# New instruction lists for all engines of a fused threshold-attention and gated-MLP kernel

## The chip, the cores and the metric

The program runs on one NeuronCore of a Trainium2 chip. The metric is the device time of one execution, in microseconds (us). The engines named below are PE (TensorE, matmuls), DVE (VectorE), ACT (ScalarE), POOL (GpSimd) and SP (SyncE, whose queue issues nearly all DMAs). PEld is the loading of matmul weights, which overlaps PE.

## The reference

Two parts, one after the other, for 8 batches of 576 tokens.

```python
# attention: 8 batches, 8 heads, 576 tokens, 64 channels per head
scores = (1 / np.sqrt(64)) * np.matmul(q, k.transpose(0, 1, 3, 2))
thresh = np.max(scores, axis=-1, keepdims=True) - tau          # tau = 0.02
scores = np.where(scores >= thresh, scores, -1e9)
attn = np.exp(scores - np.max(scores, axis=-1, keepdims=True))
attn = attn / (np.sum(attn, axis=-1, keepdims=True) + 1e-09)
x = np.matmul(attn, v)          # heads side by side: (8, 576, 512)
# gated MLP: w_in 512x1024, w_spatial 576x576, w_out 512x512
h = np.maximum(x @ w_in, 0.0)
u, v = h[..., :512], h[..., 512:]
v_n = (v - mean(v)) / np.sqrt(var(v) + 1e-06)                  # over channels
v_s = np.einsum('ts,bsd->btd', w_spatial, v_n) + b_spatial[None, :, None]
out = (u * v_s) @ w_out
```

## The kernel before

**The work.** A batch has 8 heads, taken as 4 pairs, and 18 score steps: four steps of 128 rows for each pair, and a fifth step for every second pair that does the last 64 rows of two pairs. There are 144 steps in all. The MLP of a batch follows its attention, one to three batches later, in between the score steps of later batches.

**The order is written out by hand.** `ORDER` holds four strings of tokens. String 0 is the list for batch 0, string 1 for batch 1, string 2 for batch 2, and string 3 is used for each of batches 3 to 7. `run_token` (line 884) turns a token into instructions. Each engine works through its own instructions in the order of the tokens, and waits where an operand or a buffer isn't ready. A token is a name, a colon and a lag: `es1:2` in the list of batch 5 is done for batch 3. A lag of -1 looks one batch ahead. Tokens for a batch below 0, or done already, are skipped. A `d` in front of an eviction puts it on DVE; without it the eviction is on ACT (`evict`, line 297, reads `on_vector`).

**One score step g**, by token:
- `S` and `Y` (lines 685 and 696): the score matmuls of the step, in two parts, into one of two PSUM slots (`s_ring`, two tiles). `G` between them (line 691) is an empty instruction on POOL that `Y` waits for. So PE's step can't end before POOL's queue has come to `G`.
- `M` (702): DVE takes the negative row maxima, `negm`.
- Then one of two forms, chosen by `ON_ACT`. *ACT form*: `B` (708) shifts `negm` by tau on DVE, `E` and `F` (714, the two heads) write `e` on ACT with Prelu of slope 1e30, which sends all below the threshold far down, and `Z` (737) takes the exponential of both heads on ACT. *DVE form*: `E` and `F` take the exponential on ACT, and `W` (731) is the mask on DVE: one instruction that compares `e` with exp(-tau) and multiplies.
- The slot is free for step g+2 when `E` and `F` of step g are done.

**Around it.** `QA`, `QB`, `QR` turn q, k and the last rows on PE; `qa`, `qb`, `qr` evict them (512, 512 and 128 wide); `kd`, `sq`, `sv` are POOL's copies of them and of q, k and v. `T`, `TR` (742) are the DMA transposes of the probabilities, `X`, `XR` those of the attention output; `XP`/`xp`, `RP`/`rp`, `WS`/`ws` are the same kind of turn on PE, with eviction. `P`/`p` and `R`/`r` are probabilities times v, and the division. `L` are loads; `C..` load and cast the weights.

**The MLP of a batch**: five `v` on PE, each evicted by `ev` on ACT with a sum; `n` (543) makes the mean on POOL, `k` (548) squares and sums on ACT, `N` (554) is four POOL instructions that end in the normalised `vn`. Five `u` with eviction `eu`; five `s` with the gate `es` on DVE; four `o` with eviction `eo` and `OUT`, which stores. `v4` also holds the last rows of the output of the batch before.

**After the lists** comes the tail: all that no list has done for batches 5 and 6 (`left`, line 986), then the MLP of batch 7 (`last_gmlp`, line 762), with eight PSUM banks free for it.

Of the kernel before, what the change touches and what calls it, by code (L numbers as in the profile page):

```python
# [16 lines left out]
    "L1:-1 L7:0 S0:0 G0:0 Y0:0 L0:-1 S1:0 M0:0 G1:0 Y1:0 QA1:0 L8:0 M1:0 E0:0 QR1:0 F0:0 B1:0 qa1:0 W0:0 "  # L17
    "S2:0 E1:0 G2:0 Y2:0 F1:0 dqr1:0 M2:0 Z1:0 S3:0 G3:0 kd1:0 Y3:0 E2:0 T00:0 QB1:0 M3:0 F2:0 qb1:0 B3:0 "
    "W2:0 F3:0 S4:0 E3:0 G4:0 Y4:0 Z3:0 M4:0 S5:0 Ci1:0 G5:0 Y5:0 sq2:0 L4:-1 QR2:0 B4:0 M5:0 Ci2:0 F4:0 "
    "QB2:0 E4:0 Cb0:0 dqb2:0 Z4:0 S6:0 T01:0 dqr2:0 B5:0 G6:0 sv0:0 Y6:0 F5:0 RP01:0 M6:0 QA2:0 E5:0 "  # L20
    "rp01:0 B6:0 qa2:0 QR3:0 E6:0 S7:0 G7:0 F6:0 Y7:0 M7:0 Z5:0 Ci0:0 S8:0 G8:0 kd2:0 L9:0 Y8:0 sq3:0 "
    "Z6:0 B7:0 M8:0 sv1:0 qr3:0 QB3:0 E7:0 RP00:0 B8:0 F7:0 kd3:0 T10:0 Cis1:0 drp00:0 E8:0 S9:0 F8:0 "
    "G9:0 Y9:0 Z8:0 M9:0 S10:0 G10:0 sq0:-1 Y10:0 Z7:0 B9:0 dqb3:0 Cis0:0 Cs1:0 M10:0 F9:0 QA3:0 L6:-1 "
    "R0:0 E9:0 dqa3:0 S11:0 B10:0 r0:0 G11:0 Cbs0:0 F10:0 Y11:0 P00:0 E10:0 M11:0 T11:0 sv2:0 Z9:0 S12:0 "
    "G12:0 sv3:0 B11:0 Y12:0 F11:0 P10:0 M12:0 Cis2:0 E11:0 Z11:0 Ci3:0 p00:0 L3:-1 p10:0 P01:0 Z10:0 "
    "Cs2:0 S13:0 p01:0 G13:0 sq1:-1 B12:0 Y13:0 F12:0 M13:0 T20:0 P11:0 E12:0 Css2:0 XP0:0 p11:0 dxp0:0 "
    "XP1:0 B13:0 E13:0 dxp1:0 QA0:-1 S14:0 F13:0 L2:-1 G14:0 Cis3:0 qa0:-1 Y14:0 L5:-1 QR0:-1 M14:0 "
    "QB0:-1 qr0:-1 Css4:0 XR0:0 Z12:0 S15:0 dqb0:-1 G15:0 F14:0 kd0:-1 Y15:0 P20:0 M15:0 E14:0 T21:0 "
# [1012 lines left out]
```

## Time and profile before

| | |
|---|---|
| Three runs | 450.50, 450.74, 450.67 us, median 450.67 us |
| Profiled execution | 450.5 us, of which 448.5 us is the span from the first instruction to the last |
| Granted TensorE clock | 0.996 of full speed |
| PE busy | 416.1 us (93%) |
| DVE busy | 400.8 us (89%) |
| ACT busy | 388.6 us (87%) |
| POOL busy | 176.9 us (39%) |

One instruction `M` per step marks the batches. The first `M` begins at 8.6 us; batches 1 to 7 begin theirs at 57.2, 108.7, 162.2, 213.1, 264.2, 315.2 and 366.5 us, and the last `M` ends at 414.8 us. The stretch from there to 448.5 us is called the tail here. Busy time counts an engine's instructions once where they overlap. A group of instructions is given with its count, the mean duration of one in ns, and the idle time of its engine just before it.

### The profile page before, as it was taken

How to read it: one execution, taken by the hardware profiler on the slowest of the kernel's cores; microseconds unless marked ns; L12 is line 12 of the kernel's file. 1: busy time of each engine (PE TensorE's matmuls, PEld its weight loads, DVE VectorE, ACT ScalarE, POOL GpSimd, SP SyncE). 2: the span in 40 equal slices, each digit the busy share in tenths (PEclk: the TensorE clock that was granted, in tenths of full speed). 3: DMA queues.
4: the chain of work that ended last, by engine and by line, in shares of the span. 5: the costliest groups of instructions: out<-in, count | busy, mean ns of one | idle time of the engine just before them, and what ended most of it. 6: DMA issues, size and time to landing. Idle time of an engine off the chain costs nothing.

```text
span 448.5 us, 12858 instructions
## 1 busy us (share of the span) xinstructions
PE 416.1 (93%) x5035; PEld 260.2 (58%) x5035; DVE 400.8 (89%) x615; ACT 388.6 (87%) x649; POOL 176.9 (39%) x403
## 2 busy tenths in 40 slices
PE   6776879998999899999999999999999999999995
PEld 4455556565656665666565666566665666566542
DVE  5868889899999889999999999999989999999673
ACT  3897989998989899999899988999899998999351
POOL 1256333583225724354333533255333523344021
PEclk9989999999999999999999999999999999999999
DMA  7999899899999989999999999999899996896713
GB/s 206 277 245 204 230 235 184 140 206 211 214 153 235 229 175 209 198 226 237 189 193 209 248 186 184 233 217 239 187 199 213 265 179 107 161 198 122 176 36 107
DMA packets 222556, 88.15 MB, mean 197 GB/s; under 512 B 193568, under 2 KB 218272, under 8 KB 222496
## 3 DMA queue, kind: packets, MB, share of 16 engines
q1 hardware_dynamic: 221840, 86.45, 93.5%
q8 instruction: 40, 0.66, 0.6%
q0 software_dynamic: 160, 0.52, 0.3%
q10 hardware_dynamic: 496, 0.36, 0.2%
q14 instruction: 20, 0.16, 0.1%
HBM read 32.79 MB, written 9.44 MB: 94 GB/s over the span
## 4 chain that ended last, share of the span: by engine, by line
PE 48%; DVE 24%; ACT 18%; issue 6%; POOL 2%; DMA 1%; ACTq 0%; POOLq 0%; DVEq 0%
PE s L678 20%; DVE negm L705 13%; ACT e L722 6%; ACT e L719 5%; PE f L605 5%; PE f L329 4%; PE f L576 4%; DVE p L734 3%; PE f L529 3%; PE f L381 3%; DVE xn L390 2%; ACT p L739 2%; DVE negm L711 2%; PE f L514 1%; PE f L634 1%
## 5 line engine op out<-in xcount | busy, mean ns | idle before, releaser
L705 DVE TENSOR_REDUCE negm<-s 128x2 f32<-128x1152 f32 x144 | 194.5, 1351 | 19.8 <-PE s L678 16.4
L678 PE MATMUL s<-qkT 64*64 64x160 f32 (+1 forms) x2304 | 173.2, 416 | 12.3 <-ACT e L719 7.6
L678 PEld LDWEIGHTS s<-qkT 64*64 64x64 f32 x2304 | 107.4, 132 | 67.8 <-ACT e L719 17.1
L719 ACT ACTIVATE e<-s,negm 128x576 f32<-128x576 f32 x166 | 115.3, 744 | 19.0 <-DVE negm L711 11.3
L722 ACT ACTIVATE e<-s,negm 128x576 f32<-128x576 f32 x122 | 85.8, 756 | 7.4 <-DVE negm L705 7.1
L734 DVE SCALAR_TENSOR_TENSOR p<-e,ctau 128x1152 bf16<-128x1152 f32 x61 | 86.7, 1422 | 3.5 <-ACT e L722 3.2
L739 ACT ACTIVATE p<-e 128x1152 bf16<-128x1152 f32 x67 | 78.3, 1173 | 0.4
L215 POOL CAST v<-vl 128x512 bf16<-128x512 f32 x32 | 21.0, 658 | 79.0 <-PE s L678 72.8
L381 PE MATMUL f<-v,pT 128*128 128x65 bf16 x1008 | 44.6, 194 | 0.0
L381 PEld LDWEIGHTS <-pT 128*128 128x128 bf16 x1024 | 41.6, 98 | 2.4 <-issue 0.4
L545 POOL TENSOR_SCALAR nmean<-sm 128x1 f32<-128x1 f32 (+1 forms) x35 | 16.1, 468 | 55.5 <-PE s L678 34.5
L390 DVE TENSOR_TENSOR xn<-f,r 128x256 bf16<-128x256 f32 (+1 forms) x93 | 35.4, 380 | 2.9
L605 PE MATMUL f<-wsT,vn 128*128 128x512 bf16 x135 | 33.6, 380 | 0.0
L576 PE MATMUL f<-xT,w_in 128*128 128x512 bf16 x120 | 30.8, 380 | 0.6 <-DVE xn L390 0.3
L376 PE MATMUL f<-v,pT 128*128 128x130 bf16 x126 | 27.7, 220 | 2.1 <-DVE r L388 1.5
L192 POOL COPY qn<-ql 128x512 f32<-128x512 f32 x31 | 20.1, 648 | 21.3 <-PE s L678 20.5
L561 POOL TENSOR_SCALAR vn<-vrel,rs,nm 128x512 bf16<-128x512 f32 (+1 forms) x35 | 26.8, 767 | 3.8
L529 PE MATMUL f<-w_in,xT 128*128 128x512 bf16 x112 | 27.9, 379 | 0.2 <-ACT vrel L537 0.2
L551 ACT ACTIVATE sq<-vrel,nmean 128x512 bf16<-128x512 f32 (+1 forms) x35 | 25.8, 739 | 1.7 <-POOL nmean L545 1.6
L634 PE MATMUL f<-w_o,gT 128*128 128x512 bf16 x100 | 25.0, 380 | 1.4 <-ACT qkT L309 1.4
L341 POOL COPY qkT<-qkT 64x64 f32<-64x64 f32 x32 | 7.5, 235 | 40.7 <-PE s L678 21.0
L711 DVE TENSOR_SCALAR negm<-negm 128x2 f32<-128x2 f32 x83 | 22.0, 265 | 1.7
(158 smaller groups left out, 570.8 us busy)
## 6 DMA issues: line engine op xcount, KB each, us to landing
vl<-in_v_dram SPq DMA_DIRECT2D x16, 512.0 KB, 4.9
kl<-in_k_dram SPq DMA_DIRECT2D x15, 512.0 KB, 4.8
ql<-in_q_dram SPq DMA_DIRECT2D x15, 512.0 KB, 4.9
out_dram<-oo SPq DMA_DIRECT2D x12, 512.0 KB, 4.3
uT<-in_moe_w_in_dram SPq DMA_DIRECT2D x3, 512.0 KB, 4.9
uT<-in_moe_w_spatial_dram SPq DMA_DIRECT2D x2, 576.0 KB, 4.8
vx<-in_v_dram SPq DMA_DIRECT2D x16, 64.0 KB, 3.6
pT<-p SPq DMA_TRANSPOSE x64, 5.8
```

What stands on the lines that cost most here:

```text
L381: nc.tensor.matmul(out=t[:, at + 65 * h:at + 65 * h + 65], lhsT=pt[:, 5 * h + j, :], rhs=vt[:, 6 * h + j, :], start=False, stop=(h == 1 an ...
L390: nc.vector.tensor_tensor(out=dst, in0=o[ps, g0:g1, 0:64], in1=r[ps, g0:g1].unsqueeze(2).broadcast_to([ps.stop - ps.start, g1 - g0, 64]), ...
L529: nc.tensor.matmul(out=t, lhsT=x_of(b, f, slice(c * P, (c + 1) * P)), rhs=w_in[:, f, 512:1024], start=(f == 0), stop=(f == 3))
L576: nc.tensor.matmul(out=t, lhsT=w_in[:, m, f * P:(f + 1) * P], rhs=x_of(b, m, slice(0, 512)), start=(m == 0), stop=(m == 3))
L605: nc.tensor.matmul(out=t, lhsT=vn[:, c, f * P:(f + 1) * P], rhs=wsT[:, c, 0:512], start=(c == 0), stop=(c == 4))
L678: made.append(nc.tensor.matmul(out=s_ring[g % 2][halves[k], at[h] + lo:at[h] + hi], lhsT=qks[n][halves[h], 0, m:m + 64], rhs=qks[n][halves ...
L705: nc.vector.tensor_reduce(out=nm, in_=view(s_ring[g % 2], at[0], [[at[1] - at[0], 2], [1, S]]), axis=AX.X, op=ALU.max, negate=True)
L711: nc.vector.tensor_scalar(out=nm, in0=nm, scalar1=scale if steps[g][1] == 4 else 1.0, scalar2=float(tau), op0=ALU.mult, op1=ALU.add)
L719: nc.scalar.activation(out=e, in_=s, func=ACT.Prelu, bias=bias_, scale=scale if steps[g][1] == 4 else 1.0, alpha=1e30)
L722: nc.scalar.activation(out=e, in_=s, func=ACT.Exp, bias=bias_)
L734: nc.vector.scalar_tensor_tensor(out=numerators(g), in0=ef, scalar=ctau, in1=ef, op0=ALU.is_ge, op1=ALU.mult)
L739: nc.scalar.activation(out=numerators(g), in_=e_ring[g % 3].rearrange("p h s -> p (h s)"), func=ACT.Exp)
```

## The change

All four strings of `ORDER` and the four tuples of `ON_ACT` are replaced. No function is changed. The new lists were made with evictions free to stand on DVE or ACT, and with no POOL instruction that begins together with a mask of DVE. Counted from the strings, that is from the tokens which are not skipped:

| tokens done in | batch 0 | batch 1 | batch 2 | each of 3 to 6 | tail |
|---|---|---|---|---|---|
| `u`, `v` before | 0, 0 | 5, 5 | 5, 5 | 5, 5 | 5, 5 |
| `u`, `v` after | 0, 0 | 1, 4 | 5, 5 | 5, 5 | 9, 6 |
| `s`, `o` before | 0, 0 | 1, 0 | 5, 4 | 5, 4 | 9, 8 |
| `s`, `o` after | 0, 0 | 0, 0 | 5, 0 | 5, 4 | 10, 12 |
| steps in ACT form before | 13 | 11 | 9 | 10 | |
| steps in ACT form after | 12 | 13 | 11 | 10 | |
| evictions on DVE before | 9 | 14 | 5 | 7 | |
| evictions on DVE after | 8 | 12 | 9 | 9 | |

Evictions are `qa qb qr xp rp ws eo eu` here. In each of batches 3 to 6 the nine on DVE are `eo` 2, `eu` 3, `qb` 2 and `qr` 2; before, the seven were `eo` 1, `eu` 2, `qa` 2, `qb` 1 and `qr` 1. `o` now has lag 3 where it had 2, `u1` to `u4` and `v4` lag 2 where they had 1, and their stores `OUT` go with them. The casts of `w_spatial` (`Css`) and their loads (`Cs`) move from batches 0 and 1 into batch 1; the loads and casts of `w_out` (`Co`, `Cos`) move from batches 1 and 2 into batch 2, and two of the five turns of `w_spatial` (`WS`/`ws`) from batch 1 into batch 2. The diff, with the first lines of the lists of batches 0 to 2 and the whole list of batches 3 to 7:

```diff
 ORDER = [(
-    "L1:-1 L7:0 S0:0 G0:0 Y0:0 L0:-1 S1:0 M0:0 G1:0 Y1:0 QA1:0 L8:0 M1:0 E0:0 QR1:0 F0:0 B1:0 qa1:0 W0:0 "
-    "S2:0 E1:0 G2:0 Y2:0 F1:0 dqr1:0 M2:0 Z1:0 S3:0 G3:0 kd1:0 Y3:0 E2:0 T00:0 QB1:0 M3:0 F2:0 qb1:0 B3:0 "
...
+    "Ci0:0 L7:0 S0:0 G0:0 Y0:0 L8:0 S1:0 M0:0 G1:0 Y1:0 QR1:0 Ci1:0 QA1:0 M1:0 E0:0 F0:0 B1:0 qa1:0 "
+    "dqr1:0 S2:0 W0:0 F1:0 G2:0 Y2:0 E1:0 QB1:0 Z1:0 S3:0 dqb1:0 G3:0 sv0:0 M2:0 Y3:0 T00:0 QR2:0 kd1:0 "
...
-    "RP11:1 S0:0 G0:0 Y0:0 drp11:1 WS2:1 M0:0 RP10:1 ws2:1 S1:0 rp10:1 G1:0 Y1:0 B0:0 E0:0 QR1:0 M1:0 "
-    "QA1:0 qr1:0 F0:0 qa1:0 B1:0 S2:0 W17:1 E1:0 G2:0 sq2:0 Y2:0 F1:0 QB1:0 M2:0 T31:1 Z0:0 XP2:1 S3:0 "
...
+    "S0:0 G0:0 Y0:0 RP11:1 M0:0 XP2:1 S1:0 rp11:1 G1:0 Y1:0 dxp2:1 B0:0 QB1:0 M1:0 E0:0 QA1:0 F0:0 W17:1 "
+    "E1:0 S2:0 F1:0 G2:0 Y2:0 qb1:0 T31:1 M2:0 qa1:0 QR1:0 qr1:0 QR2:0 kd1:0 S3:0 B2:0 W1:0 E2:0 G3:0 "
...
-    "S0:0 G0:0 Y0:0 XP2:1 M0:0 QR1:0 S1:0 qr1:0 xp2:1 G1:0 kd1:0 Y1:0 sq2:0 B0:0 E0:0 QB1:0 M1:0 QA1:0 "
-    "F0:0 qb1:0 S2:0 B1:0 W17:1 E1:0 G2:0 Y2:0 qa1:0 s1:2 F1:0 M2:0 T31:1 Z0:0 XP1:1 S3:0 B2:0 es1:2 G3:0 "
...
+    "u2:2 S0:0 G0:0 Y0:0 u4:2 M0:0 S1:0 eu2:2 G1:0 sq2:0 Y1:0 B0:0 deu4:2 E0:0 u3:2 M1:0 F0:0 QA1:0 Z0:0 "
+    "S2:0 B1:0 deu3:2 G2:0 Y2:0 dqa1:0 E1:0 T31:1 v4:2 M2:0 F1:0 R1:1 ev4:2 S3:0 E2:0 r1:1 G3:0 F2:0 Y3:0 "
...
-    "S0:0 G0:0 Y0:0 QA1:0 M0:0 QR1:0 qa1:0 S1:0 qr1:0 G1:0 B0:0 Y1:0 W17:1 E0:0 QB1:0 F0:0 s1:2 M1:0 "
-    "qb1:0 Z0:0 S2:0 T31:1 G2:0 es1:2 Y2:0 B1:0 s3:2 M2:0 F1:0 E1:0 R1:1 sv1:0 es3:2 S3:0 B2:0 r1:1 F2:0 "
-    "L3:-1 G3:0 kd1:0 Y3:0 sq2:0 E2:0 L1:-1 s2:2 M3:0 Z1:0 sq3:0 S4:0 B3:0 es2:2 F3:0 G4:0 Y4:0 T00:0 "
-    "E3:0 o0:2 M4:0 Z2:0 P30:1 deo0:2 S5:0 B4:0 p30:1 G5:0 E4:0 Y5:0 F4:0 QA2:0 M5:0 L0:-1 P31:1 Z3:0 "
-    "S6:0 p31:1 qa2:0 G6:0 sv2:0 Y6:0 X1:1 F5:0 o1:2 M6:0 sv3:0 E5:0 o2:2 eo1:2 W5:0 T01:0 E6:0 QB2:0 "
-    "F6:0 S7:0 eo2:2 G7:0 W6:0 Y7:0 qb2:0 S8:0 Z4:0 G8:0 sv0:0 Y8:0 M7:0 L7:-1 QR2:0 s4:2 qr2:0 L4:-1 "
-    "kd2:0 v0:1 es4:2 E7:0 M8:0 v1:1 F7:0 ev0:1 W7:0 S9:0 T10:0 ev1:1 G9:0 Y9:0 F8:0 n1:1 QR3:0 o3:2 "
-    "dqr3:0 M9:0 E8:0 v2:1 k1:1 W8:0 eo3:2 S10:0 L6:-1 ev2:1 G10:0 n0:1 TR0:0 Y10:0 E9:0 P01:0 n2:1 M10:0 "
-    "kd3:0 sq0:-1 F9:0 P00:0 k0:1 S11:0 B10:0 p01:0 F10:0 T11:0 G11:0 N0:1 p00:0 Y11:0 E10:0 QB3:0 M11:0 "
-    "v3:1 qb3:0 Z10:0 W9:0 QA3:0 S12:0 OUT3:2 ev3:1 G12:0 dqa3:0 Y12:0 E11:0 OUT1:2 v4:1 M12:0 F11:0 u1:1 "
-    "ev4:1 W11:0 T20:0 S13:0 eu1:1 n4:1 G13:0 Y13:0 B12:0 N1:1 E12:0 QR0:-1 M13:0 R0:0 qr0:-1 F12:0 "
-    "QA0:-1 k2:1 S14:0 B13:0 r0:0 G14:0 F13:0 N2:1 Y14:0 dqa0:-1 E13:0 P10:0 L8:-1 M14:0 Z12:0 P11:0 "
-    "OUT4:2 n3:1 L2:-1 S15:0 p10:0 k4:1 G15:0 kd0:-1 p11:0 Y15:0 F14:0 N4:1 u4:1 M15:0 T21:0 P20:0 eu4:1 "
-    "E14:0 u0:1 p20:0 k3:1 B15:0 W14:0 u2:1 F15:0 E15:0 S16:0 deu0:1 Z13:0 G16:0 N3:1 Y16:0 deu2:1 u3:1 "
-    "M16:0 Z15:0 X0:0 QB0:-1 sq1:-1 S17:0 eu3:1 B16:0 dqb0:-1 G17:0 E16:0 TR1:0 Y17:0 s0:1 F16:0 M17:0 "
-    "Z16:0 T30:0 P21:0 es0:1 E17:0 p21:0 F17:0 L5:-1 L9:-1 ")]
+    "S0:0 G0:0 Y0:0 QA1:0 M0:0 QB1:0 qa1:0 S1:0 W17:1 G1:0 F0:0 Y1:0 qb1:0 u1:2 M1:0 u2:2 eu1:2 E0:0 v4:2 "
+    "B1:0 deu2:2 F1:0 W0:0 T31:1 E1:0 S2:0 G2:0 ev4:2 Y2:0 o0:3 M2:0 Z1:0 QR1:0 S3:0 deo0:3 G3:0 L1:-1 "
+    "Y3:0 dqr1:0 B2:0 kd1:0 o1:3 L0:-1 F2:0 M3:0 sq2:0 E2:0 R1:1 deo1:3 Z2:0 S4:0 B3:0 r1:1 G4:0 sq3:0 "
+    "T00:0 Y4:0 F3:0 QR2:0 M4:0 P30:1 qr2:0 E3:0 P31:1 Z3:0 p30:1 S5:0 B4:0 p31:1 G5:0 sv0:0 Y5:0 F4:0 "
+    "u3:2 M5:0 E4:0 n4:2 L3:-1 QB2:0 X1:1 deu3:2 S6:0 E5:0 G6:0 dqb2:0 kd2:0 Z4:0 Y6:0 sv1:0 QA2:0 M6:0 "
+    "o2:3 sv3:0 F5:0 T01:0 qa2:0 W5:0 S7:0 F6:0 G7:0 Y7:0 E6:0 P00:0 M7:0 k4:2 S8:0 eo2:3 G8:0 N4:2 "
+    "OUT1:3 p00:0 Y8:0 F7:0 u4:2 L7:-1 M8:0 E7:0 o3:3 eu4:2 v0:1 B8:0 W6:0 eo3:3 E8:0 QB3:0 F8:0 S9:0 "
+    "W7:0 T10:0 qb3:0 G9:0 Y9:0 ev0:1 S10:0 M9:0 G10:0 Z8:0 Y10:0 QR3:0 P01:0 dqr3:0 F9:0 M10:0 kd3:0 "
+    "s0:2 TR0:0 E9:0 B10:0 S11:0 p01:0 F10:0 G11:0 n0:1 es0:2 sv2:0 L4:-1 Y11:0 E10:0 s1:2 M11:0 k0:1 "
+    "sq0:-1 T11:0 Z10:0 QA3:0 es1:2 S12:0 W9:0 qa3:0 G12:0 sq1:-1 Y12:0 F11:0 v1:1 E11:0 M12:0 P10:0 "
+    "ev1:1 L9:-1 S13:0 L6:-1 B12:0 p10:0 F12:0 G13:0 N0:1 Y13:0 E12:0 QA0:-1 M13:0 v2:1 qa0:-1 Z12:0 "
+    "T20:0 n1:1 P11:0 B13:0 W11:0 S14:0 ev2:1 G14:0 F13:0 Y14:0 p11:0 n2:1 s2:2 M14:0 E13:0 k2:1 L8:-1 "
+    "R0:0 es2:2 E14:0 L5:-1 S15:0 r0:0 Z13:0 OUT4:3 G15:0 Y15:0 QR0:-1 M15:0 v3:1 qr0:-1 F14:0 T21:0 "
+    "QB0:-1 ev3:1 B15:0 W14:0 S16:0 F15:0 G16:0 n3:1 Y16:0 k1:1 s3:2 dqb0:-1 kd0:-1 N2:1 E15:0 M16:0 "
+    "P20:0 Z15:0 L2:-1 S17:0 OUT3:3 B16:0 es3:2 F16:0 G17:0 N1:1 Y17:0 p20:0 E16:0 s4:2 k3:1 u0:1 es4:2 "
+    "M17:0 T30:0 Z16:0 N3:1 P21:0 deu0:1 F17:0 p21:0 E17:0 X0:0 TR1:0 ")]
 LAST = "W17:1 T31:1"
-ON_ACT = [(1, 3, 4, 5, 6, 7, 8, 9, 10, 11, 12, 13, 15), (0, 1, 3, 4, 6, 9, 10, 12, 13, 14, 15), (0, 1, 2, 3, 4, 8, 13, 15, 16), (0, 1, 2, 3, 4, 10, 12, 13, 15, 16)]
+ON_ACT = [(1, 3, 4, 6, 8, 9, 10, 11, 12, 13, 15, 16), (0, 2, 3, 4, 7, 8, 9, 11, 12, 13, 15, 16, 17), (0, 1, 3, 4, 10, 11, 12, 13, 14, 15, 16), (1, 2, 3, 4, 8, 10, 12, 13, 15, 16)]
```

## The prediction

> **What bounds the kernel now.** I read three views in this order: busy time by slice, busy time by stage, and the chain of waits.
>
> ```profile
> PE   6776879998999899999999999999999999999995
> DVE  5868889899999889999999999999989999999673
> ACT  3897989998989899999899988999899998999351
> ```
>
> From the eighth slice on no engine is idle for long; the spare time is at the start, and in the last three slices, where DVE and ACT fall off and PE doesn't. So I ask by stage. Below, each line is a stretch: its length, then busy time (and count) of PE, PEld, DVE, ACT, POOL, then clock and DMA. The first four are batches 0, 1, 2 and 5, the next is the tail, the last three the thirds (6 score steps each) of batch 5.
>
> ```profile
> 0.00:57.20 57.20, 41.66 (x514) 28.39 (x515) 43.55 (x80) 43.88 (x61) 21.45 (x51) 0.97 0.98 230
> 57.20:108.70 51.50, 47.66 (x615) 30.76 (x613) 47.14 (x74) 48.94 (x82) 27.00 (x56) 1.00 0.93 196
> 108.70:162.20 53.50, 50.81 (x626) 32.34 (x624) 48.54 (x69) 47.92 (x85) 22.95 (x50) 1.00 1.00 202
> 264.20:315.20 51.00, 50.17 (x618) 31.30 (x617) 48.81 (x70) 47.45 (x82) 20.70 (x49) 1.00 1.05 216
> 414.80:448.50 33.70, 27.95 (x245) 14.22 (x241) 20.46 (x51) 12.16 (x21) 4.70 (x6) 1.00 0.39 106
> 264.20:279.30 15.10, 14.95 (x182) 9.42 (x181) 14.26 (x24) 13.07 (x20) 4.14 (x10) 1.00 0.93 192
> 279.30:297.00 17.70, 17.42 (x200) 10.56 (x200) 17.12 (x19) 16.89 (x35) 7.02 (x20) 1.00 1.05 224
> 297.00:315.20 18.20, 17.80 (x240) 11.32 (x237) 17.42 (x29) 17.50 (x31) 9.53 (x21) 1.00 1.13 230
> ```
>
> Batch 5 is PE's: 50.2 of 51.0 us, with DVE (48.8) and ACT (47.5) close behind. Batches 0 to 2 are longer for reasons of their own. From the chain of waits (start, us, what), in batch 2 and in batch 5:
>
> ```profile
> 146.61 1.54 POOL rs L559
> 153.50 1.30 POOL nmean L545
> ...
> 282.43 1.42 DVE p L734
> 283.85 1.28 DVE negm L705
> 285.21 1.38 ACT e L722 x2
> 288.96 0.86 PE f L529 x4
> 289.82 1.13 PE s L678 x12
> ```
>
> The two first are POOL instructions that began inside a mask (146.31 to 147.74 and 153.25 to 154.74) and ended with it; the same two kinds take 0.55 and 0.19 us elsewhere. They are the delay that the new lists are to avoid.
>
> **Unit prices.** Successive rows of an engine overlap, so I count from start to start: `M` 1.27, `W` 1.34, two spreads 1.27, `Z` 1.06, a 512-wide eviction 0.48 on ACT and 0.60 on DVE (the rows say 0.60 and 0.68, less 0.12 and 0.08 of overlap), 128-wide 0.16 and 0.21, division `p` 0.55, gate `es` 0.60, `ev` 0.59, `k` 0.72; on PE a score step 1.13, `v`, `u`, `o` 0.86, `s` 1.08 (`u4` 0.55, `s4` 0.65), `P` 0.63, `QA` 0.55, `QR` 0.20. For each third of a batch I add what its tokens cost each engine, take the largest of the three, and add the thirds. For batch 5 that is 14.6 (PE) + 17.2 (ACT) + 17.2 (PE) = 49.0; the trace took 15.1 + 17.7 + 18.2. The sum falls short by 0.5, 0.5 and 1.0, the hand-over between engines. For batch 1 it is 15.2 + 17.8 + 16.6 = 49.6 against 51.5, for batch 2 15.1 + 16.7 + 19.0 = 50.8 against 53.5, and for batch 0 12.7 + 15.7 + 15.6 = 44.0 against 48.6 from its first `M`.
>
> **The change, part by part, against the span of 448.5 us.**
>
> *Batch 0.* Same PE work (31.0 us); one `Z` becomes a `W`. What changes is the deal: before, the middle third gave ACT 15.7 (seven `Z`) beside 10.5 for DVE. Now 12.9 + 12.7 + 14.3 = 39.9, 4.1 less. Least gain: the busiest engine, ACT, drops from 39.2 to 38.9, 0.3. I take -3.0, nearer the thirds, which had placed batches 1 and 2. `sv0` moves ahead of `G4`, behind a load of v that began at 4.6 us and took 5.5: landed long before.
>
> *Batch 1.* `u1` to `u4`, `v4`, `s0` leave: PE 44.6 to 38.9 us, ACT 48.0 to 46.2 in spite of two more `Z`. Busiest engine -1.8; thirds 14.0 + 15.0 + 17.6 = 46.6, -3.0. I take -3.0.
>
> *Batch 2.* Four `o` leave (3.44) and two turns `WS` come (0.6): PE 49.1 to 46.2; the other MLP tokens are as many as before, for an older batch. Busiest engine 49.1 to 46.3, -2.8; thirds 14.8 + 16.1 + 17.7 = 48.6, -2.2. Its last third took 21.2 us for 19.0 of work, while POOL went through `n` and `N` one after the other from 146 to 154 with the two delays above, 0.99 and 1.11. Those are worth nothing if other work waited anyway, and 2.1 if not; I take 1.0, as that third overran by 1.2 more than batch 5's. Sum -3.5.
>
> *Batches 3 to 6.* PE's work is unchanged at 48.5. DVE gains one 512-wide and one 128-wide eviction net, 0.81; ACT loses 0.64. Thirds 15.9 + 15.7 + 17.5 = 49.1 against 49.0: +0.1 each. Bounds: +0.8 each if DVE sets the pace, -0.8 each if its 2.2 us of idle time shrink to 0.6. I take +0.1, +0.4 in all. *Batch 7* the same way 48.5 to 48.6, but DVE +1.4: +0.3.
>
> *The mask rule in the steady batches.* Three POOL instructions of batch 5 lose 0.25, 0.50 and 1.09 us behind masks, but POOL is idle for 30 of 51 us, and no wait of ACT on POOL in that batch is on record: worth nothing. If the mean came late, `k`, then `N`, then `s` of the next batch would, a whole list away.
>
> ```profile
> L545 POOL TENSOR_SCALAR nmean<-sm 64x1 f32<-64x1 f32 x7 | 7.7, 1105 | 17.7 <-ACT vrel L537 17.7
> L711 DVE TENSOR_SCALAR negm<-negm 128x2 f32<-128x2 f32 x83 | 22.0, 265 | 1.7
> ```
>
> The second line is the other direction. A shift takes 0.15 us alone, yet 26 of 83 took 0.23 to 0.87, each while a copy or a normalisation ran on POOL: 8.8 us on DVE over the run, about 1.4 per steady batch. The Trainium skill ("SBUF — State Buffer", Who interferes with whom) states that DVE and GpSimd hold a port pair exclusively, and that issue order, not the shape of the operation, decides who blocks. That speaks against the change: POOL work taken out of masks must begin elsewhere, where it can begin ahead of shifts. By that rule alone, as an estimate from the 1.4 us, a steady batch could lose or win up to that much; by the rows no change. I add nothing, since the count of shifts in batches 3 to 7 stays at 50.
>
> *SP.* No DMA is added or dropped. Three `OUT` per batch move one list later, and `Cs`, `Co` likewise. Each holds SP for 0.5 us between transposes that hold it for 2.7 to 4.1; SP issues for 42.5 of 51 us in batch 5. So a transpose can be late by 0.5, and next the `P` that reads it; in the new list `P00` comes 3 steps after `T00` and `P11` 2.7 after `T11`, 7.6 us against landings of 4.6 to 7.4. Worth 0, at worst 0.5 a batch, inside the bounds above.
>
> *The tail.* It gains `v4`, `u1` to `u4`, `s0` and four `o`: 0.96 + 3.13 + 1.08 + 3.44 = 8.6 us of PE, which sets this stretch. They also fill PE's waits there:
>
> ```profile
> 419.77 0.39 PE L634 MATMUL t<-w_o,gT 128*128 128x512 bf16 x1 [0.15 <-DVE gT L619]
> 420.37 0.39 PE L634 MATMUL t<-w_o,gT 128*128 128x512 bf16 x1 [0.21 <-DVE gT L619]
> 425.07 0.28 PE L462 MATMUL t<-identb,xn 128*128 128x128 bf16 x2 [0.62 <-DVE xn L390]
> ```
>
> That is 1.0, so +7.5 (7.5 to 8.6). Their evictions stand on ACT, idle for 21 of 33.7 us: no price.
>
> Sum: -3.0 - 3.0 - 3.5 + 0.4 + 0.3 + 7.5 = -1.3. Span 447.2; the runs' median lies 2.2 above the span (450.67 against 448.5), so **449.3 us**.
>
> **The rivals.** *The tail takes it all back.* The first batches are limited by the hand-over in the two score slots, not by loads, and save only what their busiest engine drops: 0.3 + 1.8 + 2.8 = 4.9. Then -4.9 + 0.7 + 7.5 = +3.3: 454.0, slower. It decides from the point where batches 0 to 2 save less than 8.2. For it: batch 0 has 13 us of idle time on both ACT and DVE, and the thirds missed it by 4.6. Against: they met batch 1's first two thirds within 0.4.
> *DVE sets the steady pace.* +0.8 in each of five batches instead of 0.7 in all: 449.3 + 3.3 = 452.6, slower. For it: DVE busy 48.8 goes to 49.6 of 51. Against: PE still has 48.5 plus its hand-overs.
> *The steady batches gain.* Their ACT is relieved and the load of neighbouring steps is more even; DVE's floor of 49.6 plus 0.6 is 0.8 below today: five times that is 4.0, so 449.3 - 4.7 = 444.6.
> *The mask rule does nothing*: without the 1.0 and half of batch 0's gain, 451.8 - no change or just slower.
>
> **How the numbers follow.** Within 0.2% (449.8 to 451.6) is about what a measurement can't tell from no change. Forecast 0.50, of which 0.10 lies within that band; the tail 0.20; DVE's pace 0.16; steady gain 0.10; mask rule 0.04, most of it in the band. Faster 0.40 + 0.10 = 0.50, same 0.13, slower 0.37. The forecast's own range is 446.5 to 451.5; to hold eight in ten it reaches to the two rivals on either side, 444.5 to 455.0.
>
> **What would show it.** First `M` of batch 3 near 152.7 (162.2 now): later than 154 means the tail's rival. Distance of batches 3 to 6: 51.1 each; above 51.6 with DVE idle under 1.5 is DVE's pace, 50.3 the gain. Last `M` to the end: 41.2. POOL's rows for `nmean` and `rs` should have no long ones; if they do, the rule wasn't kept. I am wrong altogether if steady batches differ by more than 1 us.

## The result, and the profile after

The changed kernel takes 453.42 us, the median of 4 runs (452.01 to 453.68), beside 450.71 us for the kernel before (4 runs, 450.5 to 450.86). The ratio is 1.0054, with a 95% interval of 1.0033 to 1.0075: the change makes the kernel slower by half a per cent. The forecast was 449.3 and faster. The profiled execution of the changed kernel took 453.49 us, with a span of 451.7.

The page of the changed kernel, busy time by slice:

```profile
PE   7776688889998999999999999999999999998995
DVE  3888899997899999999999999999999999995673
ACT  2799899999998999998999989998999989997241
```

There is one more slice in which PE works and DVE and ACT don't: the end is longer. By stage, in the columns of the prediction (stretch, its length, busy time and count of PE, PEld, DVE, ACT, POOL, clock, DMA), batches 0, 1, 2 and 5 and the tail of the changed kernel are:

```profile
0.00:57.90 57.90, 42.70 (x509) 30.02 (x510) 43.60 (x78) 42.87 (x61) 19.43 (x45) 0.97 0.95 210
57.90:108.10 50.20, 42.49 (x580) 28.69 (x578) 45.11 (x72) 47.43 (x77) 26.81 (x54) 1.00 1.04 207
108.10:158.20 50.10, 47.44 (x612) 30.46 (x609) 46.56 (x71) 47.02 (x80) 23.42 (x54) 1.00 0.99 208
259.30:309.80 50.50, 49.96 (x618) 31.89 (x618) 48.78 (x74) 47.11 (x80) 21.54 (x50) 1.00 1.11 215
408.80:451.70 42.90, 35.66 (x291) 18.06 (x287) 22.73 (x54) 16.17 (x32) 8.45 (x14) 1.00 0.46 117
```

PE has 5.2 us less to do in batch 1 and 3.4 less in batch 2 than before, and 7.7 more in the tail. But batch 1 is only 1.3 us shorter, and PE now idles in it: 50.20 less 42.49. Batch 2 gave back all of the work taken out of it, batch 1 a quarter. In numbers, from the start of one batch's first maxima to the next one's (us):

| stage | before | after | difference | forecast |
|---|---|---|---|---|
| start to first maxima of batch 1 | 57.20 | 57.94 | +0.7 | -3.0 |
| batch 1 | 51.46 | 50.15 | -1.3 | -3.0 |
| batch 2 | 53.52 | 50.15 | -3.4 | -3.5 |
| batches 3 to 6, sum | 204.32 | 202.02 | -2.3 | +0.4 |
| batch 7 | 48.33 | 48.60 | +0.3 | +0.3 |
| tail | 33.62 | 42.86 | +9.2 | +7.5 |
| span | 448.5 | 451.7 | +3.2 | -1.3 |

Four terms were wrong: batches 0 and 1 (too good by 3.7 and 1.7), the tail (too good by 1.7) and the steady batches (too bad by 2.7). The first row holds more than the lists: the first maxima begin at 10.34 us here and began at 8.59 before, and in both profiles the granted clock falls to a half for 3.4 us inside batch 0, from 21.8 us before and from 18.1 us here (the third number from the end of a line is the clock). The same stretch of the changed kernel, and below it of the run with an early `TR1` (described further on), whose lists are the same up to batch 6:

```profile
18.10:21.50 3.40, 3.04 (x26) 2.33 (x30) 2.38 (x5) 2.85 (x4) 0.05 (x1) 0.50 1.31 133
```

```profile
18.10:21.50 3.40, 2.29 (x24) 1.60 (x24) 3.37 (x6) 2.46 (x4) 1.40 (x3) 1.00 1.07 124
```

So batch 0 is compared below between profiles without such a stretch. In the tail one wait can be read at once. The timeline of the changed kernel there (start, busy time, engine, line, operation, in brackets the idle time before it and what ended it; SPq is an instruction that issues a DMA):

```profile
406.01 2.74 SPq L744 DMA_TRANSPOSE pT<-p  x1
...
408.80 1.37 SPq L426 DMA_TRANSPOSE xT<-xn  x1
410.21 1.37 SPq L750 DMA_TRANSPOSE ptr<-pr  x1
412.03 3.35 SPq L744 DMA_TRANSPOSE pT<-p  x1
...
415.58 0.23 PE L375 MATMUL t<-v,ptr 128*128 128x130 bf16 x1 [2.21 <-DMA ptr<-pr]
```

`TR1`, the transpose that `ptr` is the target of, is issued third, at 410.21, and PE stands still for 2.21 us until it has landed, 5.3 us later. The chain of waits has the same: "410.21 5.32 DMA ptr<-pr". The tail before lists no wait of PE for a DMA; its last two transposes went out from 413.86, about a microsecond before the last maxima ended, and PE had other work:

```profile
413.86 7.42 SPq L745 DMA_TRANSPOSE pT<-p  x2
```

### The profile page after: what moved, and what is told of

Same layout as the page of the kernel before. It is cut to its first block, busy times and chain, and to the rows that moved or that the text cites. A ratio compares the mean times of both kernels' runs of the same rounds, so it can differ in the third digit from the quotient of the medians.

```text
span 451.7 us, 12809 instructions
## 1 busy us (share of the span) xinstructions
PE 415.9 (92%) x5035; PEld 264.5 (59%) x5035; DVE 399.8 (89%) x629; ACT 387.5 (86%) x638; POOL 182.3 (40%) x403
## 4 chain that ended last, share of the span: by engine, by line
PE 57%; DVE 21%; ACT 11%; issue 5%; DMA 5%; SPq 1%; POOL 0%; POOLq 0%; DVEq 0%; ACTq 0%
PE s L677 23%; DVE negm L704 12%; PE f L380 5%; PE f L575 4%; ACT e L718 4%; PE f L633 4%; PE f L328 3%; DVE p L733 3%; PE f L604 3%; DMA pT<-p 3%; ACT e L721 3%; PE f L528 3%; PE f L375 2%; ACT p L738 1%; PE f L513 1%
## 5 line engine op out<-in xcount | busy, mean ns | idle before, releaser
L704 DVE TENSOR_REDUCE negm<-s 128x2 f32<-128x1152 f32 x144 | 194.6, 1352 | 18.1 <-PE s L677 16.0
L677 PE MATMUL s<-qkT 64*64 64x160 f32 (+1 forms) x2304 | 174.7, 421 | 15.8 <-ACT e L721 6.4
L677 PEld LDWEIGHTS s<-qkT 64*64 64x64 f32 x2304 | 108.6, 134 | 66.3 <-ACT e L721 15.8
L733 DVE SCALAR_TENSOR_TENSOR p<-e,ctau 128x1152 bf16<-128x1152 f32 x58 | 82.1, 1423 | 0.6 <-ACT e L721 0.5
L738 ACT ACTIVATE p<-e 128x1152 bf16<-128x1152 f32 x70 | 81.6, 1170 | 1.0
L544 POOL TENSOR_SCALAR nmean<-sm 128x1 f32<-128x1 f32 (+1 forms) x35 | 11.6, 332 | 48.7 <-PE s L677 30.5
L604 PE MATMUL f<-wsT,vn 128*128 128x512 bf16 x125 | 31.1, 380 | 0.0
L191 POOL COPY qn<-ql 128x512 f32<-128x512 f32 x31 | 24.3, 784 | 15.8 <-PE s L677 15.0
L575 PE MATMUL f<-xT,w_in 128*128 128x512 bf16 x112 | 27.9, 380 | 0.7 <-ACT qkT L310 0.7
L633 PE MATMUL f<-w_o,gT 128*128 128x512 bf16 x88 | 22.7, 380 | 0.0
L328 PE MATMUL f<-identf,kn 128*128 128x128 f32 x124 | 19.1, 276 | 2.1 <-DVE negm L710 1.1
```

The costliest lines, as they stand in the source:

```text
L575: nc.tensor.matmul(out=t, lhsT=w_in[:, m, f * P:(f + 1) * P], rhs=x_of(b, m, slice(0, 512)), start=(m == 0), stop=(m == 3))
L604: nc.tensor.matmul(out=t, lhsT=vn[:, c, f * P:(f + 1) * P], rhs=wsT[:, c, 0:512], start=(c == 0), stop=(c == 4))
L633: nc.tensor.matmul(out=t[:n], lhsT=gs[b][:, f, c * P:c * P + n], rhs=w_o[:, f, :], start=(f == 0), stop=(f == 3))
L677: made.append(nc.tensor.matmul(out=s_ring[g % 2][halves[k], at[h] + lo:at[h] + hi], lhsT=qks[n][halves[h], 0, m:m + 64], rhs=qks[n][halves ...
L704: nc.vector.tensor_reduce(out=nm, in_=view(s_ring[g % 2], at[0], [[at[1] - at[0], 2], [1, S]]), axis=AX.X, op=ALU.max, negate=True)
L733: nc.vector.scalar_tensor_tensor(out=numerators(g), in0=ef, scalar=ctau, in1=ef, op0=ALU.is_ge, op1=ALU.mult)
```

## The experiments

Lengths of stages are from one profile each, times are medians. "Turn" below is that of a score slot: scores on PE (`s`), maxima (`negm`, 1.35 us) and shift on DVE, two spreads (`e`, together 1.37 us) on ACT, then the next scores in the same slot. There are two slots, so a third of a batch, 6 score steps, takes three turns. In these words the timeline of a lightened third reads so (the changed kernel with copies for transposes, described below; batch 1):

```profile
57.53 1.37 ACT L717 ACTIVATE e<-s,negm 128x576 f32<-128x576 f32 x2 [0.40 <-DVE negm L709]
...
58.95 1.20 PE L676 MATMUL s<-qkT 64*64 64x160 f32 x16 [0.65 <-ACT e L717]
...
60.29 1.36 DVE L703 TENSOR_REDUCE negm<-s 128x2 f32<-128x1152 f32 x1 [0.19 <-ACT e L720]
...
61.68 0.17 DVE L709 TENSOR_SCALAR negm<-negm 128x2 f32<-128x2 f32 x1
...
61.89 1.37 ACT L717 ACTIVATE e<-s,negm 128x576 f32<-128x576 f32 x2 [0.49 <-DVE negm L709]
```

One slot goes from spreads to spreads in 4.36 us (61.89 less 57.53): PE may write the next scores only when the spreads have read the old ones, DVE takes the maxima of what PE wrote, and ACT waits for the shift. Each of the three stands idle for a part of it (0.19 to 0.65 us in brackets), and none is full. Over that third the turns of the two slots take 1.35 + 0.45 (shift and its wait) + 1.37 + 2.10 (scores and theirs, the remainder) = 5.27 us on average; three are 15.8, about the 15.24 that the third takes. Turns follow each other, so three of them fill a third in any case: the sum shows where the time goes, and only the runs with halved passes below show that it sets the length. (The last bracket of the third row names ACT, whose spread had just ended; the maxima there need PE's scores, which ended 0.14 us before.)

**Does a second execution show the same?** The changed kernel again, with no edit.

> The new kernel once more, as it is, to stand beside the three below on one chip: 453.4 by all theories (its four runs lay between 452.0 and 453.7). Its profile began the first M at 10.34 us where the others began it at 8.6 to 8.7; a second profile shows whether that is a matter of the run (8.6 again) or of the list (10.3 again).

452.89 us (452.08 to 455.61, 6 runs; ratio 1.0057, 1.0030 to 1.0084). First maxima at 8.77 us where the first profile had 10.34, yet batch 1 begins at 57.23 (57.94). That doesn't clear the late start, since the clock differs too: this profile has three stretches of 3.4 us at half clock, from 18.6, 39.1 and 56.2 us, where the first has one. The third reaches into batch 1. Batches 1 and 2 took 50.85 and 50.41, the tail 42.36.

**The tail's wait.** `TR1` of batch 7 alone goes ahead of `T30` and `X0`:

```diff
-  "... T30:0 ... X0:0 TR1:0 ..."
+  "... TR1:0 T30:0 ... X0:0 ..."   
```

> The new lists, with the DMA transpose TR1 of batch 7 put ahead of T30 and X0 instead of behind both; nothing else moves. In the tail of the new kernel PE stands for 2.21 us until that transpose has landed (415.58 us). Theory, a late transpose is part of the tail's growth: the tail goes from 42.9 to about 40.7 us and the time from 453.4 to about 451.2. Rival, the tail is PE's work alone and the wait only moves to the next transpose: 453.4, no change. Batches 0 to 6 stay as they are.

451.0 us (448.49 to 452.26, 10 runs; ratio 0.9999, 0.9981 to 1.0016), tail 41.63. That is 0.7 to 1.2 less than in the two profiles above, but this execution spent 1.1 us more behind PE's last instruction (6.19 us; 5.04 and 5.05 there). Up to that instruction the tail falls from 37.82 and 37.31 to 35.44 us, by 1.9 to 2.4, as the theory had, and the list of waits has none of PE for a DMA. So the order on SP was worth about 2 us of the 2.7 lost. This profile has full clock throughout batch 0, and batch 1 begins at 55.54.

What PE's work in the tail is worth, the next run asks, with eight `o` of batches 5 and 6 (6.9 us of PE) left out of the tail of that kernel as well, so that two batches' output isn't complete:

```diff
+ done.update((f"o{j}", n) for j in range(4) for n in (Z - 2, Z - 1))
  rest = left(...
```

> As a_tr1 (451.0, tail 41.6 us), with the eight o products of batches 5 and 6 left out of the tail (their output rows are not computed): 32 matmuls, 8 times 0.86 = 6.9 us of PE, and nothing waits for them. Theory, PE's work sets the tail: it falls to 34.7 to 35.5 us and the time to about 444.5; so what the lists put off is paid there nearly in full. Rival, the tail is set by the chain from the last score step through transposes, x, v, statistics and gates, and the o products fill gaps: it falls by 3 us or less, to 448 or more.

447.74 us (447.13 to 448.72, 4 runs; ratio 0.9937, 0.9916 to 0.9959), tail 38.73, and 33.62 up to PE's last instruction: 6.9 us of PE work less make that only 1.8 shorter. This profile has a stretch at half clock in the tail, 416.7 to 420.1 us, which can have cost up to 1.7 us (half of 3.4, an estimate); with it added the gain is 3.5 at most. So the rival is about right. The chain of waits of this run, and its list of waits (engine, line, releaser, us in total, times, longest):

```profile
410.62 4.62 DMA pT<-p
```

```profile
PE t L445 <- DMA pT<-p: 2.3, 1, 2.3
```

Without the eight products PE stands 2.3 us before the next transpose, a wait that the run with the products doesn't have: they had filled it.

**Batch 0 alone undone.** The changed kernel with the old list for batch 0.

> The new lists of batches 1 to 7 with the old list of batch 0 (and its choice of ACT and DVE form). Theory, batch 0 is limited by hand-overs and not by loads, so its list is worth only the 0.7 us by which the two batches 0 differ (57.9 against 57.2): 452.7. Rival, the new batch 0 was to be 3 us shorter and lost that through its PSUM banks and late divisions, and batch 1 suffers from it: batches 0 and 1 together get 2 us or more shorter, 451.4 or less.

451.86 us (450.85 to 453.02, 10 runs; ratio 1.0025, 1.0013 to 1.0038), between the two. From its first maxima batch 0 took 47.8 us with the old list in this kernel, and 46.8 with the new one in the run with an early `TR1`, both at full clock:

```profile
8.70:56.50 47.80, 34.02 (x471) 22.93 (x461) 39.76 (x59) 41.07 (x57) 19.38 (x42) 1.00 1.07 238
```

```profile
8.70:55.50 46.80, 32.90 (x470) 22.63 (x463) 40.35 (x58) 39.77 (x56) 17.34 (x36) 1.00 1.06 218
```

The old list took 48.2 in the next run, again at full clock. So the new list of batch 0 saves 1.0 to 1.4 us, not the 4.1 of its loads. Each stretch at half clock adds to it: in the runs of this record with the changed list (the shift as it was, transposes or copies in place) batch 0 took 46.8 with none, 47.6 with one, and 48.2 to 48.5 with two or more. What makes the clock fall, and whether the new list makes it fall more often, was not tested.

**The steady list alone.** The kernel before, lists 0 to 2, with the changed steady list from batch 3 on.

> The old lists of batches 0 to 2 with the new list of batches 3 to 7. Batch 3 then finds nine PE tasks of its list done already (u1 to u4, v4, four o of older batches), so the lag of two is entered there and not in batches 1 and 2; the tail holds the same backlog as in the new kernel. Theory, work put off is paid in full in the tail and given back only down to the next engine's load wherever it is taken out: batch 3 falls from 50.5 to about 46, the rest is old (162.2) or new, sum about 453, the same as the new kernel within 1.5. Rival, the new lists of batches 0 to 2 are at fault: with the old ones the time falls below that of the kernel before, to 449 or less.

456.03 us (455.06 to 456.6, 4 runs; ratio 1.0118, 1.0101 to 1.0136). That is above what both gave, the theory with about 453 and the rival with 449 or less. Batch 3 then has ten PE tasks (8.6 us) fewer, since batch 2 did them by its old list:

```profile
161.70:210.80 49.10, 41.14 (x556) 28.06 (x561) 45.92 (x68) 43.85 (x71) 20.00 (x44) 1.00 1.02 203
```

PE is idle for 8 us, DVE for 3, ACT for 5, and the batch is 1.4 us shorter than a full one. This was the first sign that a lighter batch is not a shorter one.

**How short can a batch be?** The MLP of batches 0 and 1 is left out of the changed kernel (the line in `run_token`; the last output rows that ride on a `v4` go too).

```diff
+ if b < 2 and kind in ("v", "ev", "n", "k", "N", "u", "eu", "s", "es", "o", "eo", "OUT"):
+     return
  ...
```

> The new kernel with the MLP of batches 0 and 1 left out (their v, u, s, o and what hangs on them; the output rows of these batches are not computed). Batches 1, 2 and 3 then hold little but attention; by start-to-start prices the busiest engine of their thirds has 14.0, 13.9, 15.0 and 13.1, 14.7, 14.4 and 13.3, 14.5, 17.2 us. Theory, six score steps can't go below about 15 us however little else is in them, because the two score slots hand over in turn: thirds of 15.0 to 15.5 where the load is under 15, batch 1 near 47.5 and batch 2 near 46.5 us, against 50.1 and 50.0 with the MLP in. Rival, the load sets the time with the overrun of 0.5 per third of the old batch 5: batch 1 near 44.5, batch 2 near 43.7.

449.21 us. Batch 1 took 48.85, batch 2 still 50.99 with PE idle for 14.5 of it. Its chain of waits has the place:

```profile
146.03 7.94 DMA pT<-p
```

SP issued nearly back to back here, transposes of `p` holding it 2.7 to 5.3 us each. So there were two suspects: SP with its transposes, which the prediction had priced at 0, and the turn of the slots, which the first rival had named.

**SP and the transposes.** Each of the 92 DMA transposes becomes a plain DMA of the same bytes between the same tiles. PE then reads what isn't transposed, so the outputs of these kernels aren't the reference's; waits and order stay. One of the three places:

```diff
- nc.sync.dma_start_transpose(out=dst.rearrange("p c b s -> p (c b) s"), in_=...)
+ nc.sync.dma_start(out=dst.rearrange("p c b s -> p (c b s)"), in_=...)
```

> The changed kernel with each of its 92 DMA transposes replaced by a plain DMA of the same bytes between the same tiles: the waits and the order stay, but what PE then reads isn't transposed, so the output isn't the reference's. Theory (the transposes, which hold SP's queue for 2.2 to 5.3 us each and land after 3.3 to 7.9, keep the lightened batches 1 and 2 at 50 us): with copies that hold it for 0.6 us these two fall by 2 us or more each, below the 50.5 of the steady batches, and the tail loses its wait of 2.2 us for the last transpose. Rival (hand-overs between PE, VectorE and ScalarE inside each score step keep them): batches 1 and 2 stay within 0.7 of 50.15 and only the tail gets shorter.

> The kernel before with the same replacement of its 92 transposes by copies; its output isn't the reference's either. With the run of the changed kernel with copies beside it: if the transposes are why the change brought 4 us in batches 0 to 2 and not the 9.5 that the loads give, the changed kernel with copies is faster than this one by about 1.3 us (9.5 less 7.5 in the tail, less 0.7 elsewhere) or by more; if not, it stays slower by 2 to 3 us, as with transposes (453.4 against 450.7).

> The run that leaves out the MLP of batches 0 and 1, with copies in place of the transposes as well. Theory (transposes and SP's queue): batch 2, 50.99 us with PE idle for 14.5, falls to 46 or less, and batch 1, 48.85, to 46 or less. Rival (hand-overs within a score step): batch 1 stays at 48 or above, and batch 2 loses only the wait for a transpose in its last third, so 48 to 49.

> The changed kernel with its 92 DMA transposes left out: PE reads tiles that were filled once at the start. No wait of PE for a DMA of these is left, and SP has loads and stores alone; the output isn't the reference's. It bounds what transposes can cost in any way. If batches 1 and 2 stay within 0.5 of 50.15 us, the transposes have nothing to do with their length and a chain on PE, VectorE and ScalarE sets it; if they fall by 2 us or more each, the transposes set it. Batches 3 to 6 stay at 50.5, within 0.3, in both theories, since PE is idle for only 0.5 of them.

The changed kernel with copies takes 449.84 us (448.45 to 451.0, 10 runs; ratio 0.9985 to the kernel before, 0.9972 to 0.9999), the kernel before with copies 450.33 (449.89 to 451.8, 10 runs; 0.9997, 0.9985 to 1.0009). So transposes cost the changed kernel 3.1 to 3.6 us (against its two medians) and the kernel before 0.3, which is within its interval. But they are not what holds batches 1 and 2:

```profile
55.70:105.80 50.10, 42.42 (x578) 28.63 (x576) 45.10 (x71) 47.34 (x77) 26.77 (x54) 1.00 0.64 207
105.80:155.80 50.00, 47.39 (x612) 30.46 (x610) 46.66 (x71) 46.80 (x79) 23.45 (x54) 1.00 0.64 209
```

Batches 1 and 2 are as long as with transposes (50.15 each), with the DMA engines at 0.64 where they were at 1.04 and 0.99. My theory for them fell here. What the profiles show of that cost lies in the tail: 35.44 up to PE's last instruction for 37.82, and the wait for `ptr` is gone. That is what the early `TR1` alone gives, to 0.01 us. In batch 0 they cost nothing: 46.81 here and 46.82 with transposes and an early `TR1`, both at full clock; that batch 1 begins at 55.73 here and at 57.94 in the first profile goes with its late start and its half clock. The clock also stands between the medians, since the ten executions of the changed kernel were granted 0.985 to 0.999 and those with copies 0.995 or 0.999; but the one at 0.999 took 452.08, and the three with copies at 0.999 448.45 to 448.87. About 1 us of that isn't placed.

In the run without MLP in batches 0 and 1, copies (444.24 us) take batch 2 from 50.99 to 47.36, all of it in its last third (20.09 to 16.47; up to 1.6 of it is a stretch at half clock at the end of that third with transposes), and batch 1 stays at 48.86: as the rival said for batch 1, and 0.6 better for batch 2. With the transposes left out altogether, batches 1 and 2 take 51.06 (its start is at half clock for 3.4 us) and 50.09, 3 to 6 50.4 to 50.7. The time of that kernel, 463.87, means nothing, since filling the tiles at the start delays the first maxima to 22.8 us.

**The turn of the two slots.** On the kernel with copies, one kind of pass at a time covers only half of its columns in batches 1 and 2 (so their output isn't the reference's), for example the spreads:

```diff
- s = view(s_ring[g % 2], at[h], [[1, S]])
+ n = S // 2 if g // 18 in (1, 2) else S
+ s = view(s_ring[g % 2], at[h], [[1, n]])
```

> The changed kernel with copies in place of transposes, and in batches 1 and 2 the spreads of scores cover half of their columns: about 0.24 us less each (a 1152-wide pass of ScalarE takes 1.17 us and a 576-wide one 0.69), 36 of them a batch, so ScalarE loses 8.6 us a batch, and each turn of a score slot loses 0.48. Theory (the turn of the two slots sets the light thirds): 9 turns a batch, 4.3 us less where nothing else binds; batches 1 and 2, 50.1 and 50.0 us, fall to 46 to 48. Rival (loads of PE or VectorE, or other hand-overs): they lose less than 1.0 us each.

> The same kernel with full spreads, but in batches 1 and 2 the second exponentials on ScalarE cover half of their columns: 24 in the two batches, 0.48 us less each, so ScalarE loses 6.2 and 5.3 us a batch, none of it inside the turn of a slot. Theory (the turn): batches 1 and 2 lose less than 1.0 us each, and less than half of what the halved spreads bring. Rival (ScalarE's load sets them): each loses 3 us or more, in proportion to the load taken off about two thirds of what the halved spreads bring.

> The same kernel with full spreads and exponentials, but in batches 1 and 2 the masks on VectorE cover half of their columns: 5 and 7 of them, from 1.44 to about 0.75 us, so VectorE loses 3.4 and 4.8 us, outside the turn except that a mask can stand ahead of a shift in VectorE's order. Theory (the turn): each batch loses 0 to 1.5 us, only by shifts that come earlier. Rival (VectorE's load sets them): 3 us or more each.

> The changed kernel with copies in place of transposes, and in batches 1 and 2 the maxima of scores taken over half of their columns: from 1.35 us to about 0.75, 18 a batch, so each turn of a slot and each step of VectorE loses 0.6. Theory (the turn of a slot with VectorE's maxima as its longest part sets the light thirds): 9 turns by 0.6 are 5.4 us; after the halved spreads gave 40 and 15% of their sum, at least 2 us for each of batches 1 and 2. Rival (some other chain, as evictions and PE's order): less than 1 us each, as with the masks.

> Maxima and spreads of batches 1 and 2 both over half of their columns: the turn loses 1.1 us, 9.7 a batch, and no engine but PE keeps its load. Theory (the turn): batch 1 ends near what PE alone would take, 38.9 us by unit prices with 1 to 3 us of hand-over, so 40 to 44 us; batch 2 near 46.2 with the same, 47 to 49. Rival: no more than the sum of the two separate runs.

| halved in batches 1 and 2 | in the turn | off the engine, batch 1 and 2 | batch 1 | batch 2 |
|---|---|---|---|---|
| nothing | | | 50.10 | 50.00 |
| second exponentials | no | ACT 4.9 and 5.2 | 49.77 | 50.26 |
| masks | no | DVE 2.4 and 2.3 | 50.12 | 51.02 |
| spreads | yes | ACT 8.2 and 7.6 | 48.37 | 49.31 |
| maxima | yes | DVE 9.6 and 9.7 | 47.37 | 47.38 |
| maxima and spreads | yes | both | 44.32 | 46.43 |

The single times were, in the order of the rows from the second, 450.45, 449.57, 448.58, 446.36 and 440.66 us. The load taken off an engine outside the turn (ACT 5 us, DVE 2.4) brings 0.3 us at most, and batch 2 even gets longer; in the turn it brings something, and both parts together bring 5.8 us in batch 1, more than the sum of the two (1.7 and 2.7). The spreads alone gave less than the 4.3 I had from nine turns. Where the maxima stay, DVE seems to be next: from 66 to 82 us they make up 46% of the chain of waits with halved spreads, and 24% with full ones. In the window of batch 2 with both halved

```profile
101.20:147.60 46.40, 45.92 (x605) 30.49 (x608) 37.07 (x72) 38.75 (x79) 22.92 (x54) 1.00 0.68 226
```

PE is busy for 45.92 of 46.40: now PE's load sets the length, and it is what the unit prices had given for it (46.2). It is a little less than the 47 to 49 I expected; batch 1 took 44.3, just above its 40 to 44, with 2.6 us of PE idle. So the sum of PE's work was right in batch 2; it just didn't bind. Batch 1's last third is a case of its own: 19.45 us with copies, 17.49 with both halved, for a load of 17.6 by unit prices; what else holds it was not separated.

**The shift blocked by POOL.** In the kernel before, with two edits: where the negated maxima go for a step on ACT is a pair of columns of the score slot in PSUM, and the shift reads them there.

```diff
+ if on_act(g):
+     nm = s_ring[g % 2][:, 0:2]
  nc.vector.tensor_reduce(out=nm, ...
- nc.vector.tensor_scalar(out=nm, in0=nm, ...
+ nc.vector.tensor_scalar(out=nm, in0=s_ring[g % 2][:, 0:2], ...
```

> The kernel before, with one edit: in ACT-form steps the row maxima are written to two spare columns of the score slot in PSUM and the shift reads them there, so that the shift has an operand in PSUM and at most one in SBUF. Theory, the shifts' 8.8 us of blocked time behind POOL copies and normalisations (26 of 83 shifts over 0.2 us) go, 1.4 us of VectorE per steady batch, and a steady batch falls from 51.0 to about 50.5, as in the new lists, which have 4.5 us of it: 448.3. Rival, PE sets the steady pace and hides them: 450.7, or slower by what PSUM access adds.

447.48 us (446.48 to 447.71, 4 runs; ratio 0.9923, 0.9905 to 0.9941): better than both kernels. The shift's rows in the changed kernel and in this one (x count, busy, mean ns):

```profile
L710 DVE TENSOR_SCALAR negm<-negm 128x2 f32<-128x2 f32 x86 | 18.5, 215 | 2.0
```

```profile
L715 DVE TENSOR_SCALAR negm<-s 128x2 f32<-128x2 f32 x83 | 12.9, 156 | 1.7
```

Before, 83 shifts took 22.0 us, 265 ns each. Read from PSUM they take 156 and none is long; batches 3 to 6 fall from 51.0 to between 50.38 and 50.75. The changed kernel with this edit and the early `TR1`:

> The new lists with TR1 of batch 7 ahead of T30 and with the shift reading the maxima in PSUM. In the new lists only 4.5 us of shift time is blocked behind POOL, one shift of 0.52 us in each steady batch, against 8.8 us before. Theory, the new lists' faster steady batch (50.5 against 51.0) came from fewer blocked shifts, so here the edit brings at most the remaining 0.4 a batch, and less where PE sets the pace: 451.0 less 1 to 2, 449 to 450. Rival, it is worth the same 3.1 us as with the old lists: 447.9.

448.19 us (446.2 to 452.3, 10 runs; ratio 0.9952, 0.9927 to 0.9977). That is 2.8 less than with the early `TR1` alone, nearer to the rival's 3.1 than to the theory's 1 to 2. But the gain isn't in the steady batches, which stay at 50.45, where the change alone had 50.48 to 50.60. Between the two profiles, both at full clock in the batches, batch 0 falls from 46.82 to 45.41 us and batch 1 from 50.11 to 49.32: by 1.4 and 0.8, where the long shifts (over 0.2 us) had lost 1.6 and 0.8. So there a delay of the shift, which is a part of the turn, was paid nearly in full; batch 2 gained 0.2 for 0.5.

## Why the prediction was wrong, step by step

**Batches 0 and 1: the step that failed.** The prediction took each third's busiest engine for the third's length and let batches 0, 1 and 2 shrink by 9.5 us in all. They shrank by 4.0. The thirds of batch 1 were to take 14.0 + 15.0 + 17.6 = 46.6 before hand-overs and took 15.24 + 15.45 + 19.46 = 50.15, with PE idle for 7.7. The check of the unit prices had given a sign: they fell short by 0.5 to 1.0 a third in batch 5, which PE filled, but by 4.6 in batch 0, which no engine filled, and the forecast subtracted loads there all the same. Lightened, a third meets the turn of the two slots, which is a chain through PE, DVE and ACT and no engine's load. The runs with halved passes show it for batches 1 and 2, with the last third of batch 1 as said. Batch 0 took 14.4 + 15.4 + 17.0 at full clock for loads of 12.9 + 12.7 + 14.3, and 1.0 to 1.4 less than with the old list where the forecast had 3.0; that shorter shifts shorten it too (1.4 for 1.6) speaks for the same cause, but no pass was halved there. The rest of the +0.7 in the table is the late first maxima and the clock.

**Batch 2** came out as forecast, -3.4 for -3.5, in part by luck, since halved maxima shorten it by 2.6: the turn limits it too, and not the loads alone. The 1.0 in it for the mask rule is neither confirmed nor refuted. The two delays that it stood for are gone: no `rs` or `nmean` in batch 2 takes over 0.6 us now. In the whole kernel the rule doesn't hold: 36 POOL instructions began inside a mask after the change and 33 before, and they are longer than others of their kind by 20 us in all (16.5 before). The list orders instructions, and these rows show that it doesn't fix when they start. POOL's share of the chain that ends last is 0% now and was 2%, so most of these delays lie off the path. The rival "The mask rule does nothing" isn't settled by these runs.

**Steady batches.** I had +0.1 each and -0.8 as a bound; they gained 0.45 to 0.8, although DVE is busier with evictions. The prediction named the blocked shifts as a risk of 1.4 us either way and added nothing. After the change 13 of 86 shifts took over 0.2 us and lost 4.5 us, before 26 of 83 and 8.8. In each of batches 3 to 6 the long shifts lost about 1.25 us before and 0.32 after; in batches 0 and 1 they lose more than before. Taking all of it away in the kernel before, by the shift in PSUM, is worth 0.6 per steady batch, so fewer blocked shifts are enough to give the gain. That it came by them is argued: with both there is nothing further to gain (50.45), but PE, idle for only 0.5 of 50.5 us, would stop any other gain there too. That the new order, and not the freed evictions, thinned out the blocked shifts was not separated.

**The tail** was mis-sized by 1.7. The work itself was near: with copies in both kernels it costs 6.9 (40.59 against 33.66), and with an early `TR1` 6.5 up to PE's last instruction (35.44 against 28.90), less than the 7.5. The rest is PE's wait for `TR1`, 2.2 us in the first profile and 1.7 in the second, and that comes from the step "*SP.* ... Worth 0, at worst 0.5 a batch": I looked at the three `OUT` and not at what stands last on SP. Moving `TR1` alone ends the wait.

**The rivals.** "The tail takes it all back" gave 454.0 by way of batches "limited by the hand-over in the two score slots, not by loads", and this is the mechanism that the runs with halved passes show. Its sign came too: the first `M` of batch 3 began at 158.2 us, where later than 154 was to mean this rival. Its size was nearly right by accident: batches 0 to 2 saved 4.0 for its 4.9, the tail cost 1.7 more, and the steady batches gained what neither had. Against it I had held that the thirds met batch 1's first two within 0.4; they did, before, when those thirds were full by their loads (15.2 and 17.8).

Of the 2.7 us that the kernel lost, the one wait for `TR1` accounts for about 2; with copies in both kernels the changed one is level or 0.5 us ahead. It is no more than that because 8.6 us of PE work went to a tail where they cost 6.5 to 6.9, and batches 1 and 2, which they left, gave 4.7: PE could idle there under the turn's length.

## What to carry to other kernels

A sum of loads tells the length of a stage only while one engine is full; before taking work out of a stage, find the shortest turn of its buffers (here maxima, shift, spreads and scores in two slots), since below it the work taken out only becomes idle time, and still costs where it is put. When work is moved to the end of a kernel, look for the last transfer there and what PE can do until it has landed. A small instruction that is held up by another engine in the middle of a chain (the shift, 0.16 us by itself) can be worth more than the evening out of an engine's load. And before a difference between two profiles is given to a change, look at the granted clock in the stage where it lies.

## What the runs showed of the hardware

A shift of 128x2 took 265 ns on average over the kernel before, with its operand in SBUF, and 156 when it read the operand from PSUM; the two kernels take 450.6 and 447.5 us. Of the 83 shifts before, 57 took 149 to 171 ns. The other 26 took 228 to 871 ns; each began inside a copy or a normalisation of POOL, and 25 of them ended 0.02 to 0.03 us after it did. The Trainium skill ("SBUF — State Buffer", Who interferes with whom) counts tensor_scalar among the operations that can take the port pair that DVE and GpSimd share, if their operands meet certain conditions, and says that the second to issue blocks fully. The rows agree: the long shifts last to the end of POOL's instruction, and none was long once it read PSUM. The granted clock fell to 0.50 for 3.4 us at a time, none to three times in batches 0 to 2 of the kernels above; one such stretch in batch 0 made it 0.8 us longer (47.6 for 46.8). Why it falls was not tested. A transpose of `p` holds the queue that issues it for 2.4 to 5.6 us in the changed kernel (median 3.3), a plain DMA of the same bytes for about 0.5; yet with SP issuing for 43.8 of 50.5 us in batch 5 (16.5 with copies), the steady batches are no shorter with copies (50.48 us with both). What loads issued from a queue other than SP's would bring was not measured.
